# One transfer instead of two for the first step's second pair of q and k, and its split in two operations

## The chip, the cores and the metric

The kernel runs on one core of one Trainium2 chip. The metric is the device time of one execution in microseconds (us); the kernel before takes 1039.08 us, the median of 3 runs (1039.03 to 1039.14). The engines of the core work side by side, each through its own list of instructions in order, and wait for one another through semaphores: PE (TensorE, matrix multiplication; its weight loads are shown apart as PEld), DVE (VectorE, elementwise), ACT (ScalarE, elementwise and functions by table), POOL (GpSimd) and SP (SyncE, which here only issues transfers). Transfers between the chip's main memory and the core's own memory (DMA) are issued by SP or ACT, each into a queue of its own, and carried out by 16 DMA engines.

## The reference

With q, k and v of shape 8 x 12 x 448 x 64 in float32, the attention is a sigmoid one, and its result goes through a feed-forward network with squared ReLU:

```python
scores = scale * np.matmul(q, k.transpose(0, 1, 3, 2)) - np.log(S)
attn = 1.0 / (1.0 + np.exp(-scores))
attn_out = np.matmul(attn, v)
x = np.ascontiguousarray(attn_out.transpose(0, 2, 1, 3)).reshape(B * S, H * D)   # 3584 x 768
h = x @ w_in                       # 768 x 2048
r = np.maximum(h, 0.0)
g = s * (r * r) + b
out = g @ w_out                    # 2048 x 768
```

## The kernel before

The time falls into the attention, the network for a first block of 512 tokens (with weights still being prepared), and the network for two groups of three token blocks each, done by a scheme with fewer block products. Only the start of the attention is touched by the change.

**Steps.** The attention runs over 24 steps, the list `quads`: 8 batches times 3 groups of four heads. One step holds the four heads as two pairs. In a step's tile `x = ld_[0]` of shape [128, 2, 2, 448] the 128 partitions are two heads of 64 dimensions, the second axis is the pair (0 or 1), the third tells q (0) from k (1), the last is the position. So `x[:, 0, 0]` is the first pair's q, `x[:, 0, 1]` its k, `x[:, 1]` the second pair's q and k together, which lie behind one another both in the tile and in main memory: 2 x 448 float32, 3584 bytes a partition.

**High and low parts.** TensorE multiplies plain float32 slowly; a product of numbers rounded to a shorter float32 form (`F32R`) is faster. The kernel therefore splits an operand into a rounded high part and the remainder, the low part, and adds three products, in the order of `PARTS` (line 39): high weights by high data, high weights by low data, low weights by high data. The tiles are `qkh` and `qkl`. They cover, for each pair, the 448 columns of q and the first 384 of k (`NX = S + 3 * P` = 832 columns; `flat` gives this view).

For most steps the split is made by ScalarE (`parts_hi`) and VectorE (`parts_lo`). For the first two steps VectorE makes both (`parts_dve`, lines 390 to 396): for each piece of the list it is given, first a cast (line 394), then a subtraction (line 395, shown in the profile under the helper's line 181).

**Scores.** `scores` (lines 403 to 434) makes six blocks of scores a step: pair `i` in 0, 1 and block `c` in 0 to 2 of 128 positions of k. Each block has two heads, on the two halves of the partitions. In the first step the blocks (0,0) and (0,1) are made of plain float32 straight from the transferred tile (line 426), because the parts aren't there yet; (0,2), (1,0), (1,1) and (1,2) are made in parts (line 420). TensorE takes them in this order. ScalarE makes the sigmoid of each block (line 400). The last 64 positions of k follow later, in `scores_last` (line 441), then the products with v in `attn_v` (line 454) and `attn_v_last` (line 463).

**What is issued first.** `load(..., first=True)` (lines 358 to 368) issues the first step's q and k in five transfers on two queues:

- SP: k of pair 0, the first 128 columns (line 361)
- ACT: q of pair 0 (line 362)
- SP: k of pair 0, the rest (line 363)
- ACT: q of pair 1 (line 364)
- SP: k of pair 1 (line 365)

Then SP issues v of the first step (line 372), q and k of the second step in one transfer (line 367), the first rows of the weights (line 503), v of the second step and two small vectors. ACT, once its transfers are issued, loads its function table and does one tiny operation (line 476). TensorE runs eight warm-up multiplications on constants (line 482, tile `idle`), which need no transfer.

VectorE splits the first step in four pieces (line 594), in this order: q of pair 0; q of pair 1; the last third of pair 0's k that is split (for block (0,2)); k of pair 1. Each piece is a cast and a subtraction, so eight instructions. Tile buffers are in pairs for q and k (`ld`, line 349) and single for the parts (`hl`, line 350).

The order of everything is written out by hand: the loop at line 595 emits the instructions in the order in which each engine takes them, with the preparation of weights placed at given steps (`at_step`, `ticks`).

Of the kernel before, what the change touches and what calls it, by code (L numbers as in the profile page):

```python
# [94 lines left out]
def sigmoid_attention_relu2_ffn(  # L95
# [10 lines left out]
    nc = tc.nc  # L106
    B, NQ, P, _, _, S = qk.shape
# [66 lines left out]
    def f32(ap):  # L174
        return ap.bitcast(F32)
# [4 lines left out]
    def sub(o, x, y):  # L180
        nc.vector.tensor_tensor(o, x, y, op=ALU.subtract)  # L181
# [173 lines left out]
    quads = [(b, t) for b in range(B) for t in range(NQ)]  # L355
    NL = len(quads)

    def load(b, t, first=False):
        x = ld.tile([P, 2, 2, S], F32, tag="qk", name=f"qk_{b}_{t}")
        if first:  # L360
            nc.sync.dma_start(x[:, 0, 1, :P], qk[b, t][:, 0, 1, :P])
            nc.scalar.dma_start(x[:, 0, 0], qk[b, t][:, 0, 0])
            nc.sync.dma_start(x[:, 0, 1, P:], qk[b, t][:, 0, 1, P:])
            nc.scalar.dma_start(x[:, 1, 0], qk[b, t][:, 1, 0])
            nc.sync.dma_start(x[:, 1, 1], qk[b, t][:, 1, 1])
        else:
            nc.sync.dma_start(x, qk[b, t])
        return [x]
# [6 lines left out]
    NX = S + 3 * P  # L375

    def flat(x):
        return x.rearrange("p i x s -> p i (x s)")[:, :, :NX]
# [11 lines left out]
    def parts_dve(b, t, ld_, pieces):  # L390
        hi, lo = (hl.tile([P, 2, NX], F32R, tag=h, name=f"qk{h}_{b}_{t}") for h in "hl")
        x = flat(ld_[0])
        for i, cols in pieces:
            nc.vector.tensor_copy(hi[:, i, cols], x[:, i, cols])
            sub(lo[:, i, cols], x[:, i, cols], f32(hi[:, i, cols]))
        ld_.append((hi, lo))
# [71 lines left out]
    def store_x(b, t, pav):  # L468
        o = xo.tile([P, 2, S], F32, tag="xo", name=f"xo_{b}_{t}")
        nc.vector.tensor_copy(o, pav[:, :, :S])  # L470
        nc.sync.dma_start(x_dram[b][:, 2 * t : 2 * t + 2], o)

    loaded = {0: load(*quads[0], first=True)}
    load_v(*quads[0], loaded[0])
    loaded[1] = load(*quads[1])
    nc.scalar.activation(e_bias, nls, AF.Sigmoid)
    nc.vector.memset(e_bias, -896.0 * 2.0**23)
# [113 lines left out]
    at_step(NL - 2, "ACT", 8, lambda: w1.append(base_hi(0, 0)))  # L591
    at_step(NL - 1, "DVE", 1, lambda: base(0, 0, w1[0]))

    parts_dve(*quads[0], loaded[0], [(0, slice(S)), (1, slice(S)), (0, slice(S + 2 * P, NX)), (1, slice(S, NX))])
    for n, (b, t) in enumerate(quads):
        if n:
            ticks(n, "DVE")
# [15 lines left out]
        if n + 2 < NL:  # L613
            loaded[n + 2] = load(*quads[n + 2])
# [336 lines left out]
    for n, blocks in enumerate(threes):  # L951
# [258 lines left out]
        for j, (i, p) in enumerate(L2):  # L1210
# [8 lines left out]
            for e, tk in LAST if end else [(e, slice(TB)) for e in range(KC)]:  # L1219
# [11 lines left out]
                if end:  # L1231
                    x = C["t"][:, e, tk]
# [57 lines left out]
```

## Time and profile before

| | |
|---|---|
| time, median of 3 runs | 1039.08 us |
| the profiled execution's own time | 1039.04 us |
| its span, first to last instruction | 1037.2 us |
| matrix instructions (PE) | 5290, as many weight loads (PEld) |
| VectorE, ScalarE instructions that count as busy | 910, 666 |
| granted TensorE clock | 1.000 |
| the feed-forward of the two groups of three blocks begins at | 381.35 us |
| shares of the chain by the attention: lines 454, 420, 441, 463 | 11%, 9%, 2%, 2% |

How to read the profile's views. The page gives busy time and share of the span of each engine, and the chain of work that ended last, followed back from the last instruction. The timeline lists instructions in order of time: start in us from the span's start, duration in us, engine, line, operation, the tile written and the tiles read, their shape, the count, and in brackets the idle time of the engine before it and what ended it. An engine name with q (SPq, ACTq) is that engine's issuing of a transfer, which doesn't count as busy; the duration there is that of the issue and not of the transfer. The DMA view gives for each issuing line the size of one transfer and the time from issue to landing. A releaser in brackets is inferred: where several things were waited for it is the one that came last by the profile, and "issue" means that nothing the profile shows was waited for.

### The profile page before, as it was taken

How to read it: one execution, taken by the hardware profiler on the slowest of the kernel's cores; microseconds unless marked ns; L12 is line 12 of the kernel's file. 1: busy time of each engine (PE TensorE's matmuls, PEld its weight loads, DVE VectorE, ACT ScalarE, POOL GpSimd, SP SyncE). 2: the span in 40 equal slices, each digit the busy share in tenths (PEclk: the TensorE clock that was granted, in tenths of full speed). 3: DMA queues.
4: the chain of work that ended last, by engine and by line, in shares of the span. 5: the costliest groups of instructions: out<-in, count | busy, mean ns of one | idle time of the engine just before them, and what ended most of it. 6: DMA issues, size and time to landing. Idle time of an engine off the chain costs nothing.

```text
span 1037.2 us, 13906 instructions
## 1 busy us (share of the span) xinstructions
PE 1033.5 (100%) x5290; PEld 780.9 (75%) x5290; DVE 837.3 (81%) x910; ACT 617.0 (59%) x666; POOL 0.2 (0%) x4
## 2 busy tenths in 40 slices
PE   9999999999999999999999999999999999999998
PEld 4545555555888888888888888888888888888887
DVE  5999999995988965898898897796455789888777
ACT  7999999988776755564445344344445335552432
POOL 0000000000000000000000000000000000000000
PEclk9999999999999999999999999999999999999999
DMA  9788989994999999999686676897666666676773
GB/s 334 265 333 340 359 321 393 345 398 190 338 362 366 358 409 410 340 341 322 201 267 190 218 230 219 292 317 249 197 192 194 194 192 196 191 233 212 221 227 119
DMA packets 101569, 287.17 MB, mean 277 GB/s; under 512 B 10240, under 2 KB 20352, under 8 KB 101504
## 3 DMA queue, kind: packets, MB, share of 16 engines
q1 hardware_dynamic: 101216, 285.84, 79.3%
q8 instruction: 42, 0.69, 0.3%
q10 hardware_dynamic: 288, 0.46, 0.1%
q14 instruction: 23, 0.19, 0.0%
HBM read 198.18 MB, written 88.08 MB: 276 GB/s over the span
## 4 chain that ended last, share of the span: by engine, by line
PE 100%; DVE 0%; issue 0%
PE o L1225 31%; PE h L1095 31%; PE pav L454 11%; PE psc L420 9%; PE ph L563 6%; PE po L765 6%; PE psc_l L441 2%; PE pav L463 2%; PE idle L482 0%; PE psc L426 0%; DVE C_t L181 0%
## 5 line engine op out<-in xcount | busy, mean ns | idle before, releaser
L1095 PE MATMUL h<-s_0h,wu 128*128 128x512 f32 x480 | 148.0, 389 | 0.0
L1095 PE MATMUL h<-s_1h,wu 128*128 128x512 f32 x480 | 147.8, 389 | 0.0
L400 ACT ACTIVATE a<-psc,nls 128x896 f32<-128x896 f32 x144 | 132.7, 1008 | 12.9 <-PE psc L420 10.1
L454 PE MATMUL pav<-a,v 128*64 128x448 f32 x576 | 113.8, 543 | 0.0
L1095 PEld LDWEIGHTS h<-s_0h,wu 128*128 128x128 f32 x480 | 90.1, 188 | 18.8
L1095 PEld LDWEIGHTS h<-s_1h,wu 128*128 128x128 f32 x480 | 90.1, 188 | 18.6
L968 ACT COPY G<-h 128x1024 f32<-128x1024 f32 x48 | 48.8, 1017 | 85.4 <-PE h L1095 57.7
L860 ACT ACTIVATE G<-G,b_sb,s_sb 128x1024 f32<-128x1024 f32 x48 | 59.8, 1246 | 61.4 <-DVE G L857 60.7
L1095 PE MATMUL h<-s_0l,wu 128*128 128x512 f32 x240 | 93.4, 389 | 0.0
L1095 PE MATMUL h<-s_1l,wu 128*128 128x512 f32 x240 | 93.4, 389 | 0.0
L454 PEld LDWEIGHTS pav<-a,v 128*64 128x64 f32 x576 | 39.1, 137 | 63.8 <-issue 45.4
L178 DVE TENSOR_TENSOR G<-G,h 128x1024 f32<-128x1024 f32 x40 | 48.8, 1219 | 39.1 <-PE h L1095 38.9
L1225 PE MATMUL o<-g_3h,wu 128*128 128x512 f32 (+1 forms) x244 | 79.0, 385 | 0.0
L1225 PE MATMUL o<-g_1h,wu 128*128 128x512 f32 x240 | 78.8, 389 | 0.0
L1225 PE MATMUL o<-g_2h,wu 128*128 128x512 f32 x240 | 78.8, 389 | 0.0
L1225 PE MATMUL o<-g_0h,wu 128*128 128x512 f32 x240 | 78.8, 389 | 0.0
L765 PE MATMUL po<-g,w 128*128 128x512 f32 x288 | 67.7, 389 | 0.0
L765 PEld LDWEIGHTS po<-g,w 128*128 128x128 f32 x288 | 54.1, 188 | 11.2
L563 PE MATMUL ph<-x0h,w 128*128 128x512 f32 x192 | 61.7, 390 | 0.0
L420 PE MATMUL psc<-qkh 64*128 64x448 f32 x284 | 54.8, 382 | 0.0
L1225 PEld LDWEIGHTS o<-g_3h,wu 128*128 128x128 f32 x244 | 45.6, 188 | 9.2
L1225 PEld LDWEIGHTS o<-g_0h,wu 128*128 128x128 f32 x240 | 45.1, 188 | 9.4
(152 smaller groups left out, 2029.7 us busy)
## 6 DMA issues: line engine op xcount, KB each, us to landing
wu<-wd SPq DMA_DIRECT2D x240, 512.0 KB, 3.8
wd<-t SPq DMA_DIRECT2D x36, 768.0 KB, 8.1
qk<-qk_t SPq DMA_DIRECT2D x23, 896.0 KB, 7.1
st<-w_out SPq DMA_DIRECT2D x16, 768.0 KB, 9.3
st<-w_in SPq DMA_DIRECT2D x16, 768.0 KB, 9.2
wd<-w SPq DMA_DIRECT2D x16, 768.0 KB, 5.9
v<-v_t SPq DMA_DIRECT2D x24, 448.0 KB, 5.4
xd<-xo SPq DMA_DIRECT2D x24, 448.0 KB, 4.4
```

Source lines behind the costliest of these rows:

```text
L178: nc.vector.tensor_tensor(o, x, y, op=ALU.add)
L400: nc.scalar.activation(a, psc[:, :, :S], AF.Sigmoid, bias=nls, scale=SCALE)
L420: nc.tensor.matmul(o[:, j, :S], two[wi][r, i, cols], two[xi][r, i, :S], start=m == 0, stop=m == 2,)
L441: nc.tensor.matmul(psc[half[i], j, :S], x[r, i, 1, 3 * P :], x[r, i, 0, :], start=True, stop=True,)
L454: nc.tensor.matmul(pav[r, i, :S], ld_[1][:, 3 * i + c, j, :], a[i, c][:, j, :], start=c == 0, stop=False,)
L463: nc.tensor.matmul(pav[r, i, :S], ld_[1][half[i], 6, j, :], a[half[i], j, :], start=False, stop=True,)
L563: nc.tensor.matmul(ph, w[:, k, wi, kc * P : (kc + 1) * P], x0[h][xi][:, cc, :], start=m == 0, stop=m == 3 * NCC - 1,)
L765: nc.tensor.matmul(pos[e], w[:, k, wi, kc * P : (kc + 1) * P], g[:, gi, :], start=first and i == 0, stop=last and i == 2,)
L860: nc.scalar.activation(x, x, AF.Identity, bias=b_sb, scale=s_sb)
L968: nc.scalar.copy(g(m, h), bk)
L1095: nc.tensor.matmul(bk[:, j], wt[:, j, wi, c * P : (c + 1) * P], opd[i][xi][:, c, :], start=i == ch[0] and m == 0, stop=m == 3 * KC - 1, sk ...
L1225: nc.tensor.matmul(o, wt[:, f, wi, e * P : (e + 1) * P], g[gi][:, f, tk], start=(end or i == ch[0] and p == 0) and f == 0 and m == 0, stop ...
```

## The change

In `load`, the two transfers of pair 1 (q on ACT's queue, k on SP's) become one transfer of `x[:, 1]`, both, on SP's queue, at the place where k of pair 1 was. ACT's queue keeps q of pair 0 alone. In the split on VectorE, the piece for block (0,2) moves ahead of pair 1, and pair 1's two pieces become one of 832 columns: three pieces, six instructions.

```diff
@@ -361,8 +361,7 @@
             nc.sync.dma_start(x[:, 0, 1, :P], qk[b, t][:, 0, 1, :P])
             nc.scalar.dma_start(x[:, 0, 0], qk[b, t][:, 0, 0])
             nc.sync.dma_start(x[:, 0, 1, P:], qk[b, t][:, 0, 1, P:])
-            nc.scalar.dma_start(x[:, 1, 0], qk[b, t][:, 1, 0])
-            nc.sync.dma_start(x[:, 1, 1], qk[b, t][:, 1, 1])
+            nc.sync.dma_start(x[:, 1], qk[b, t][:, 1])
         else:
             nc.sync.dma_start(x, qk[b, t])
         return [x]
@@ -591,7 +590,7 @@
     at_step(NL - 2, "ACT", 8, lambda: w1.append(base_hi(0, 0)))
     at_step(NL - 1, "DVE", 1, lambda: base(0, 0, w1[0]))
 
-    parts_dve(*quads[0], loaded[0], [(0, slice(S)), (1, slice(S)), (0, slice(S + 2 * P, NX)), (1, slice(S, NX))])
+    parts_dve(*quads[0], loaded[0], [(0, slice(S)), (0, slice(S + 2 * P, NX)), (1, slice(NX))])
     for n, (b, t) in enumerate(quads):
         if n:
             ticks(n, "DVE")
```

The arithmetic of every element is the same. Behind line 364 the line numbers of the changed kernel are one smaller.

## The prediction

> **What bounds the kernel now.** I read the first page from the top: busy times first, then the chain of work that ended last.
>
> ```profile
> span 1037.2 us, 13906 instructions
> PE 1033.5 (100%) x5290; PEld 780.9 (75%) x5290; DVE 837.3 (81%) x910; ACT 617.0 (59%) x666; POOL 0.2 (0%) x4
> PE 100%; DVE 0%; issue 0%
> ```
>
> The reader is to see that TensorE is the bound over the whole span: it is busy for 1033.5 of 1037.2 us and the chain is all PE. So the change can move the end only by moving a time at which TensorE starts or waits; time saved or lost on VectorE, ScalarE or a queue counts only where TensorE stood behind it. Conversely, a stall of TensorE near the start is not made up later, because no slack stands behind it in the chain.
>
> The change touches the first 8 us alone, so the second view is the chain restricted to the first 40 us.
>
> ```profile
> 0.77 3.15 PE idle L482 x8
> 3.92 2.98 PE psc L426 x8
> 6.90 2.43 PE psc L420 x24
> 9.33 2.41 PE pav L454 x12
> ```
>
> The first column is the start, the second the duration. The eight warm-up matmuls (`idle`) run to 3.92, the plain fp32 scores of blocks (0,0) and (0,1) to 6.90, the scores in parts, (0,2) and (1,0) to (1,2), to 9.33, then attention times v. Each piece starts where the one before ends: TensorE never stops between 0.77 and 9.33. The question is whether each instruction's operands still arrive in time.
>
> Third, the timeline of the first 3 us: who issues which transfer (start, duration of the issue, queue).
>
> ```profile
> 0.72 0.41 ACTq L362 DMA_DIRECT2D qk<-qk_t  x1
> 0.73 0.38 SPq L361 DMA_DIRECT2D qk<-qk_t  x1
> 1.16 0.45 ACTq L364 DMA_DIRECT2D qk<-qk_t  x1
> 1.17 0.42 SPq L363 DMA_DIRECT2D qk<-qk_t  x1
> 1.64 0.42 SPq L365 DMA_DIRECT2D qk<-qk_t  x1
> 1.65 1.28 ACT L476 ACT_TABLE_LOAD   x1 [1.65 <-PEq L1280]
> 2.10 0.43 SPq L372 DMA_DIRECT2D v<-v_t  x1
> ```
>
> L362 is the first q (q0), L361 and L363 the two pieces of the first k (k0a, 128 columns; k0b, the rest), L364 the second q (q1), L365 the second k (k1). Fourth, the DMA view restricted to the first 2.5 us: size of each and time from issue to landing.
>
> ```profile
> qk<-qk_t ACTq DMA_DIRECT2D x2, 224.0 KB, 3.2
> v<-v_t SPq DMA_DIRECT2D x1, 448.0 KB, 5.3
> qk<-qk_t SPq DMA_DIRECT2D x1, 224.0 KB, 4.1
> qk<-qk_t SPq DMA_DIRECT2D x1, 160.0 KB, 3.5
> qk<-qk_t SPq DMA_DIRECT2D x1, 64.0 KB, 2.6
> ```
>
> With the issue times: k0a lands at 0.73 + 2.6 = 3.33, k0b at 1.17 + 3.5 = 4.67, k1 at 1.64 + 4.1 = 5.74, v at 2.10 + 5.3 = 7.40. Fifth, VectorE, which splits q and k into high and low parts.
>
> ```profile
> 3.58 0.40 DVE L394 CAST qkh<-qk 128x448 fp32r<-128x448 f32 x1 [0.32 <-DMA qk<-qk_t]
> 4.01 0.62 DVE L181 TENSOR_TENSOR qkl<-qk,qkh 128x448 fp32r<-128x448 f32 x1
> 4.82 0.40 DVE L394 CAST qkh<-qk 128x448 fp32r<-128x448 f32 x1 [0.18 <-DMA qk<-qk_t]
> 5.25 0.62 DVE L181 TENSOR_TENSOR qkl<-qk,qkh 128x448 fp32r<-128x448 f32 x1
> 5.79 0.22 DVE L394 CAST qkh<-qk 128x128 fp32r<-128x128 f32 x1
> 6.04 0.29 DVE L181 TENSOR_TENSOR qkl<-qk,qkh 128x128 fp32r<-128x128 f32 x1
> 6.25 0.35 DVE L394 CAST qkh<-qk 128x384 fp32r<-128x384 f32 x1
> 6.64 0.56 DVE L181 TENSOR_TENSOR qkl<-qk,qkh 128x384 fp32r<-128x384 f32 x1
> 9.77 0.59 DVE L394 CAST qkh<-qk 128x832 fp32r<-128x832 f32 x1 [2.58 <-DMA qk<-qk_t]
> 10.40 1.03 DVE L181 TENSOR_TENSOR qkl<-qk,qkh 128x832 fp32r<-128x832 f32 x1
> ```
>
> The pairs are q0, q1, the last third of k0 used by (0,2), and k1. The last two rows are half of the next step's split: a cast and a subtraction of 832 columns, exactly the form that the change makes of the q1 and k1 pairs. Last, the weight loads of TensorE, which show when the operands are needed.
>
> ```profile
> 4.75 0.34 PEld L426 LDWEIGHTS psc<-qk 64*128 64x128 f32 x2 [0.41 <-DMA qk<-qk_t]
> 5.50 0.34 PEld L426 LDWEIGHTS psc<-qk 64*128 64x128 f32 x2 [0.41 <-issue]
> 6.25 0.30 PEld L420 LDWEIGHTS psc<-qkh 64*128 64x128 f32 x2 [0.41 <-DVE qkh L394]
> 6.74 0.19 PEld L420 LDWEIGHTS psc<-qkl,qkh 64*128 64x128 f32 x2 [0.19 <-issue]
> 6.94 0.19 PEld L420 LDWEIGHTS psc<-qkh,qkl 64*128 64x128 f32 x2
> 7.14 0.19 PEld L420 LDWEIGHTS psc<-qkh 64*128 64x128 f32 x2
> 7.34 0.20 PEld L420 LDWEIGHTS psc<-qkl,qkh 64*128 64x128 f32 x2
> 7.54 0.20 PEld L420 LDWEIGHTS psc<-qkh,qkl 64*128 64x128 f32 x2
> ```
>
> The loads at 4.75, 5.50 and 6.25 stand 0.75 us apart, each after the same 0.41 of idle time, though three releasers are named. The one in the middle waited for nothing the profile shows, so 0.75 is TensorE's own pace for an fp32 round, and the DMA and VectorE named at the other two had just come in time. The three loads from 6.25 are (0,2); those at 7.14, 7.34 and 7.54 are (1,0): high by high, high weights against low q, low weights against high q. After that the pace is 0.20 us a round.
>
> **The change, part by part.** All sums stand against the profiled execution's own 1039.04 us (span 1037.2, 1.84 around it), 0.04 under the median of 1039.08 of the runs.
>
> *ScalarE's queue loses the transfer at 1.16.* It saves 0.45 us of issue there, so the table load may begin at about 1.2 instead of 1.65. Worth nothing, because ScalarE's first real work waits for TensorE:
>
> ```profile
> 5.76 1.01 ACT L400 ACTIVATE a<-psc,nls 128x896 f32<-128x896 f32 x1 [2.62 <-PE psc L426]
> 6.95 4.60 ACT L400 ACTIVATE a<-psc,nls 128x896 f32<-128x896 f32 x5 [0.19 <-PE psc L426]
> ```
>
> The cover is the 2.62 us of idle time before 5.76. Without it the saving could count for at most its 0.45 us.
>
> *SyncE's queue.* The third transfer carries 448 KB instead of 224. Its issue should cost the same: 0.42 us for 224 KB at 1.64, 0.43 for v's 448 KB at 2.10. So v and everything issued behind it (the next step's q and k, the weight rows) is issued when it was. The bytes ahead of v are the same, so v still lands near 7.40, before attention times v at 9.33; cover 1.9 us.
>
> *When does the joint transfer land?* It is not in the trace; this is the disputed term. From below, k0b's 3.5 us give 1.64 + 3.5 = 5.14. From above, v, issued just behind it, landed 5.3 us after its issue; the same for the joint transfer gives 1.64 + 5.3 = 6.94. I take 4.1 us, that of k1, hence 5.74: k1 was issued at that very place, and when it had landed the same bytes as now had to be in: 64 + 160 + 224 on SyncE's queue and twice 224 on ScalarE's, 896 KB. The change reorders them and takes none away.
>
> One page of the Trainium skill says otherwise. "DMA: Bandwidth & Descriptors", section "Anatomy of one DMA — SWDGE (gpsimd) path", gives a transfer as 2.0 us fixed plus its bytes at 436 GB/s. It is stated for the other path's transfers; an estimate by it is 2.0 + 1.05 = 3.05 us for 448 KB, a landing at 4.69, and then the sum below would be zero. The trace does not bear it out for transfers queued behind others: the same estimate for k1's 224 KB is 2.5 us, and its row has 4.1.
>
> *VectorE's order.* New order: q0 (high, low), the last third of k0, then q1 and k1 as one cast and one subtraction of 832 columns. q0 ends at 4.01 + 0.62 = 4.63, k0b is in at 4.67, so the k0 third runs from about 4.7 to 4.7 + (6.33 - 5.79) = 5.24 instead of 6.33. TensorE gains nothing, since (0,2) cannot start before its own pace lets it, at 6.25. Four instructions become two, and 0.40 + 0.62 + 0.35 + 0.56 = 1.93 us become 0.59 + 1.03 = 1.62. That saving is also off the path: after this VectorE waits 2.58 us for the next q and k until 9.77, and neither the bytes ahead of that transfer nor its issue time change.
>
> *The new wait.* Before, the low part of q1 was ready at 5.87, and k1's at 6.64 + 0.56 = 7.20, asked for at 7.54. Now both come out of one subtraction, so the load at 7.34 waits for it. From the rows at 9.77 and 10.40, cast start to end of the subtraction is 0.63 + 1.03 = 1.66; the cast starts some 0.02 to 0.1 after landing. Landing at 5.74 gives 5.79 + 1.66 = 7.45, against a need at 7.34. High parts are no concern (5.79 + 0.59 = 6.38, needed at 7.14). TensorE then waits 7.45 - 7.34 = 0.11 us. What stands behind it on TensorE are the rest of (1,0), (1,1), (1,2) and attention times v, all in its own order, so all of them move by 0.11. ScalarE does not: its third and fourth sigmoids follow one another in the run of five from 6.95, at about 0.92 us each, the fourth of all at 6.95 + 2 x 0.92 = 8.8 for (1,0), which TensorE, with its last weight load at 7.54 and 0.20 us a round, ends near 8.0; cover some 0.7 us. SyncE's next load into this tile waits for the later subtraction too, but also for TensorE's last scores from the tile, which stand behind attention times v in TensorE's order and so come later.
>
> Sum: 0 (queues) + 0 (saved VectorE time) + 0 ((0,2) earlier) + 0.11 (new wait) = +0.11 us, hence 1039.04 + 0.11 = 1039.15. By the bounds of the landing time the wait is 0 (landing 5.14: the subtraction ends at 6.85) to 8.65 - 7.34 = 1.31 us (landing 6.94).
>
> **Rivals.** *A: no wait at all.* If the joint transfer lands before 5.63 (7.34 less 1.66 and 0.05), TensorE never sees it: 1039.04. For it speaks that 5.63 is within 0.11 us of my 5.74, and half as many, longer rows might move a little faster; against it, that k1 at the same place needed 4.1 us. Should the joint transfer in fact be cut into the same pieces as before, so that nothing differs but the queue, the time is this one too.
>
> *B: slower, a late landing.* The one subtraction now stands behind the last byte of both halves, so any delay of that transfer goes one to one into TensorE from a landing at 5.63 on. If it takes as long as v did, the wait is 1.31 us and the time 1040.35. For it: v's row shows that 448 KB on this queue at this time did need 5.3 us; against it: v lay behind all 896 KB, the joint transfer is the end of them. It decides as slower by over 0.2% only if the landing came at 5.63 + 2.08 = 7.71, beyond v's own.
>
> *C: faster, an earlier start.* With q1 gone from ScalarE's queue, q0 and k0b have less beside them. If TensorE's first scores waited for q0 (its load at 3.84 does name a DMA), they start earlier, and everything with them:
>
> ```profile
> 3.84 0.51 PEld L426 LDWEIGHTS psc<-qk 64*128 64x128 f32 x4 [0.73 <-DMA qk<-qk_t]
> ```
>
> ScalarE's two transfers have 3.2 us in the middle; q1, which VectorE saw at 4.82, took some 3.6 from 1.16, so q0 took about 2.8 and landed at 0.72 + 2.8 = 3.52. The most that rival C can give is q0 as early as k0a, at 3.33: 0.19 us, so 1038.85. Against it: VectorE saw q0 at 3.58, a quarter of a microsecond before that load, and the warm-up matmuls hold TensorE to 3.92 anyhow. k0b coming earlier gives nothing, as its load at 4.75 was at TensorE's pace. The rule behind this rival is in the same page of the Trainium skill, section "Queues, rings and completion order": each DMA engine takes turns between the queues that have work, so one queue less leaves larger shares to the other. No row here shows the turns themselves.
>
> **How the numbers follow.** Forecast (a wait of 0.02 to 0.6 us): 0.53. Rival A: 0.30, as its bound is so near. Rival B (over 0.6 us): 0.09. Rival C: 0.08. The range takes in the forecast's waits, A and C, each with the spread of the runs (1039.03 to 1039.14): 1038.8 to 1039.8; what it leaves out is B and a little of what nobody named. Faster or slower by over 0.2%, which is 2.08 us and about what a measurement of this kernel can tell from no change, would need a landing after 7.71 or a start earlier by ten times what C offers: 0.01 and 0.03, and 0.96 for within it.
>
> **What would show it.** In the profile after: three issues on SyncE's queue at 0.73, 1.17 and 1.64 and one on ScalarE's; the table load near 1.2; the k0 third's cast near 4.7; one cast of 832 columns at the landing plus 0.02 to 0.1, with idle time before it put down to the DMA; the second and third rounds of (0,2) at 6.74 and 6.94 as before; and the low-q round of (1,0) at 7.34 plus the wait, its load naming the subtraction. A landing before 5.63 without a wait is A. I am wrong if TensorE's rounds before 7.14 move, if the wait is over 0.6 us, or if the time moves by more than the first 10 us account for.

## The result and the profile after

The changed kernel is slower: 1040.45 us, the median of 21 runs (1039.80 to 1041.37), against 1038.86 for the kernel before (21 runs, 1038.45 to 1040.25). The ratio is 1.0016 with a 95% interval of 1.001 to 1.0022. That is within the 0.2% named in the prediction, but outside the range of 1038.8 to 1039.8. The profiled execution took 1040.38 us, 1.34 more than the one of before, where the forecast was 0.11.

The first page: TensorE is still nearly all of the chain, but a transfer has entered it.

```profile
span 1038.6 us, 13902 instructions
PE 1034.1 (100%) x5290; PEld 780.6 (75%) x5290; DVE 837.0 (81%) x908; ACT 617.1 (59%) x666; POOL 0.2 (0%) x4
PE 99%; DMA 0%; DVE 0%; SPq 0%; issue 0%
```

The chain of the first 40 us (start, duration) shows where:

```profile
1.58 0.05 issue
1.64 5.02 DMA qk<-qk_t
6.65 0.02 issue
6.68 0.61 DVE qkh L393
7.28 0.02 issue
7.31 1.04 DVE qkl L181
8.34 0.04 issue
8.39 1.91 PE psc L419 x15
10.30 2.41 PE pav L453 x12
```

Where the chain of before ran along TensorE from the first warm-up, this one runs from the issue of the joint transfer at 1.64 through its landing at 6.65, the cast and the subtraction to TensorE at 8.39. The products with v begin at 10.30 for 9.33: 0.97 us is lost here.

The transfers of the first 2.5 us, size and time to landing:

```profile
qk<-qk_t SPq DMA_DIRECT2D x1, 448.0 KB, 5.0
v<-v_t SPq DMA_DIRECT2D x1, 448.0 KB, 6.5
qk<-qk_t ACTq DMA_DIRECT2D x1, 224.0 KB, 2.8
qk<-qk_t SPq DMA_DIRECT2D x1, 160.0 KB, 2.8
```

k0b lands sooner than before (2.8 us for 3.5); the joint transfer takes 5.0, where k1 at the same place took 4.1. VectorE's new order and TensorE's weight loads:

```profile
4.53 0.22 DVE L393 CAST qkh<-qk 128x128 fp32r<-128x128 f32 x1
6.68 0.60 DVE L393 CAST qkh<-qk 128x832 fp32r<-128x832 f32 x1 [1.61 <-DMA qk<-qk_t]
7.31 1.03 DVE L181 TENSOR_TENSOR qkl<-qk,qkh 128x832 fp32r<-128x832 f32 x1
```

```profile
6.12 0.19 PEld L419 LDWEIGHTS psc<-qkh 64*128 64x128 f32 x2 [0.28 <-issue]
6.49 0.19 PEld L419 LDWEIGHTS psc<-qkl,qkh 64*128 64x128 f32 x2 [0.19 <-issue]
6.70 0.18 PEld L419 LDWEIGHTS psc<-qkh,qkl 64*128 64x128 f32 x2
7.39 0.22 PEld L419 LDWEIGHTS psc<-qkh 64*128 64x128 f32 x2 [0.51 <-PE psc L419]
8.39 0.19 PEld L419 LDWEIGHTS psc<-qkl,qkh 64*128 64x128 f32 x2 [0.78 <-DVE qkl L181]
```

VectorE waits 1.61 us for the transfer, and the low-q round of (1,0) names the subtraction, at 8.39 where it had stood at 7.34. The low-part rounds of block (0,2) run 0.25 us earlier than before (6.49 and 6.70 for 6.74 and 6.94), which the prediction had excluded.

A second loss stands far from the change. ScalarE's first sigmoid of the fifth step, in the profile of before and then of after:

```profile
48.20 3.73 ACT L400 ACTIVATE a<-psc,nls 128x896 f32<-128x896 f32 x4 [0.58 <-PE psc L420]
```

```profile
49.48 1.91 ACT L399 ACTIVATE a<-psc,nls 128x896 f32<-128x896 f32 x2 [0.89 <-PE psc L419]
```

It starts 1.28 us later than before, though TensorE is only 0.97 late there (its scores of that step begin at 48.27 for 47.30). TensorE then waits for ScalarE (0.30 us in the scores, 0.39 before the products) and ends up about 0.35 us later still: its main stage, the feed-forward of the two groups, begins at 382.67 for 381.35, so 1.32 of the 1.34 us.

### The profile page after: what moved, and what is told of

Read it like the earlier page. It is cut to its first block, busy times and chain, and to the rows that moved or that the text cites. A ratio compares the mean times of both kernels' runs of the same rounds, so it can differ in the third digit from the quotient of the medians.

```text
span 1038.6 us, 13902 instructions
## 1 busy us (share of the span) xinstructions
PE 1034.1 (100%) x5290; PEld 780.6 (75%) x5290; DVE 837.0 (81%) x908; ACT 617.1 (59%) x666; POOL 0.2 (0%) x4
## 4 chain that ended last, share of the span: by engine, by line
PE 99%; DMA 0%; DVE 0%; SPq 0%; issue 0%
PE o L1224 31%; PE h L1094 31%; PE pav L453 11%; PE psc L419 9%; PE ph L562 6%; PE po L764 6%; PE psc_l L440 2%; PE pav L462 2%; DMA qk<-qk_t 0%; DVE qkl L181 0%; DVE qkh L393 0%; DVE C_t L181 0%; SPq L363 0%; SPq L361 0%
## 5 line engine op out<-in xcount | busy, mean ns | idle before, releaser
L419 PE MATMUL psc<-qkl,qkh 64*128 64x448 f32 x284 | 52.0, 363 | 0.5 <-DVE qkl L181 0.5
```

Of the source, the lines that this page charges most:

```text
L419: nc.tensor.matmul(o[:, j, :S], two[wi][r, i, cols], two[xi][r, i, :S], start=m == 0, stop=m == 2,)
```

## The experiments

Asked in turn: is it the transfer or the split; what makes the transfer late; is that accident or rule; what the loss at 49 us is. "Products" is the start of the first products with v in the timeline: 9.27 before, 10.23 after.

**The split alone** (transfers as before).

```diff
-    parts_dve(..., [(0, slice(S)), (1, slice(S)), (0, slice(S + 2 * P, NX)), (1, slice(S, NX))])
+    parts_dve(..., [(0, slice(S)), (0, slice(S + 2 * P, NX)), (1, slice(NX))])
```

> Transfers as before (five, two queues), the split on VectorE as after (q0, the third of k0, then q1 and k1 in one cast and one subtraction). Two theories of the lost time. S: the joint transfer is late because its first rows of 3584 bytes start slowly, as v's did in the trace before. Q: it is late because everything now stands in one queue. Both say here that nothing of the lateness is left: k1 lands some 4.1 us after its issue (5.7), the joint subtraction ends at 7.4, the products with v begin between 9.1 and 9.4 (before 9.27, after 10.23), and the time is within 0.2 us of before. A rival to both, that the joint split itself costs the time: the products begin after 9.8.

k1 took 4.3 us (landing 5.94), the subtraction ended at 7.65, and the products began at 9.53, a little past the 9.4 expected: landing, 1.66 of VectorE, and TensorE, the prediction's sum with 0.2 us more of landing. Median 1039.33, ratio 1.0004 (0.9995 to 1.0013): not told from no change. So the split is not what costs the 0.97 us. It is not free either: here TensorE's low-q round waited for the joint subtraction, to 7.71, and the products stood 0.26 us later than before.

**The transfer alone** (split as before).

```diff
-            nc.scalar.dma_start(x[:, 1, 0], qk[b, t][:, 1, 0])
-            nc.sync.dma_start(x[:, 1, 1], qk[b, t][:, 1, 1])
+            nc.sync.dma_start(x[:, 1], qk[b, t][:, 1])
```

> The joint transfer on SyncE's queue as after, VectorE's four pieces in the order of before (q0, q1, third of k0, k1). What is asked is whether the landing is late with the old split too, and what the new order saves. The transfer lands 4.8 to 5.2 us after its issue (6.4 to 6.8); the third of k0 now stands behind q1, so block (0,2) waits for the transfer as well: its low part comes 1.5 us after the landing and k1's 0.8 to 0.9 later. The products with v begin at 10.4 to 10.9 (after 10.23). A rival, that the joint split had made the transfer's cost worse: they begin before 10.1.

Landing after 4.9 us, products at 10.63, 1040.71 us, ratio 1.0018 (1.0008 to 1.0028). The whole loss comes with the transfer; the new split, in one profile of each, gives 0.4 us of it back, as (0,2) no longer stands behind q1 on VectorE.

**Two transfers on SyncE's queue.**

```diff
-            nc.sync.dma_start(x[:, 1], qk[b, t][:, 1])
+            nc.sync.dma_start(x[:, 1, 0], qk[b, t][:, 1, 0])
+            nc.sync.dma_start(x[:, 1, 1], qk[b, t][:, 1, 1])
```

> As after, but q1 and k1 are two transfers of 224 KB one behind the other on SyncE's queue (rows of 1792 bytes); ScalarE's queue has q0 alone; v is issued one place later. S: the rows are small, so no slow start: k1, issued at 2.1, lands at 5.3 to 5.9, and the products with v begin at 9.0 to 9.4; time within 0.3 us of before. Q: one queue is what is slow: k1 lands at 6.3 to 7.0, the products begin at 9.9 to 10.5; time 0.7 to 1.6 us above before.

**The joint transfer on ScalarE's queue.**

```diff
-            nc.sync.dma_start(x[:, 1], qk[b, t][:, 1])
+            nc.scalar.dma_start(x[:, 1], qk[b, t][:, 1])
```

> As after, but the joint transfer is issued on ScalarE's queue behind q0, at 1.16, where q1 was. S: rows of 3584 bytes start slowly wherever they stand: landing about 5 us after the issue, 6.1 or later, and the products with v begin at 9.7 or later. Q: two queues are in use again, so it lands as q1 and k1 did before, 4.8 to 5.6, and the products begin at 9.0 to 9.3.

S falls twice; Q's landings hold both times. With small rows but one queue, k1 landed at 2.10 + 4.71 = 6.81 and the products began at 10.44 (1040.64 us, ratio 1.0016, 1.0007 to 1.0025). With the large rows on ScalarE's queue the transfer landed 3.9 us after its issue, and VectorE began with it at once (the chain's transfer of 3.95 from 1.17, the cast):

```profile
1.17 3.95 DMA qk<-qk_t
5.11 0.02 issue
5.14 0.60 DVE qkh L393
```

Products at 8.66, 1038.83 us, ratio 1.0 (0.999 to 1.0009): the loss is gone. That they began earlier than Q's 9.0 is TensorE's pace in this profile (last section), and the median shows no gain. What the DMA engines moved shows the difference too. Each row is half a microsecond: the busy time of PE, PEld, DVE, ACT and POOL, then the granted clock, the DMA share and GB/s; first after, then this kernel:

```profile
3.50:4.00 0.50, 0.50 (x4) 0.16 (x2) 0.41 (x2) 0.00 (x0) 0.00 (x0) 1.00 1.03 206
4.00:4.50 0.50, 0.50 (x2) 0.35 (x4) 0.50 (x1) 0.00 (x0) 0.00 (x0) 1.00 1.01 280
4.50:5.00 0.50, 0.50 (x4) 0.25 (x2) 0.47 (x3) 0.00 (x0) 0.00 (x0) 1.00 0.79 201
```

```profile
3.50:4.00 0.50, 0.50 (x4) 0.16 (x2) 0.39 (x1) 0.00 (x0) 0.00 (x0) 1.00 1.06 423
4.00:4.50 0.50, 0.50 (x2) 0.35 (x4) 0.48 (x1) 0.00 (x0) 0.00 (x0) 1.00 0.99 401
4.50:5.00 0.50, 0.50 (x6) 0.27 (x4) 0.47 (x3) 0.00 (x0) 0.00 (x0) 1.00 1.06 430
```

After moves bytes at about half the rate, while the DMA engines are nearly as busy: the packets took longer (112 from 3.5 to 5.0 us in after, 213 in this kernel). The joint transfer alone is not the reason, for the kernel before slows down too, one microsecond later:

```profile
4.50:5.00 0.50, 0.50 (x4) 0.24 (x2) 0.32 (x2) 0.00 (x0) 0.00 (x0) 1.00 1.68 283
5.00:5.50 0.50, 0.50 (x2) 0.10 (x2) 0.47 (x2) 0.00 (x0) 0.00 (x0) 1.00 0.51 179
```

In both kernels the stretch begins when ScalarE's queue has run dry: the DMA view shows no packet of it from 4.5 us on in before and from 3.5 us on in after. The Trainium skill, "DMA: Bandwidth & Descriptors", section "Issuing engines are not separate DMA queues", says that issuing from several engines saves only the issue time, as all share the same DMA engines. Here the issue was 0.47 us earlier and the landing 1.5 us (5.12 for 6.65), so more than the issue time was saved in these first microseconds. Whether the other queue did it is not shown by this kernel alone: the transfer also stands second in its queue and no longer third. The experiments on the place in the queue, below, take that up.

**The third of k0 earlier, four pieces** (transfers as before).

```diff
-    parts_dve(..., [(0, slice(S)), (1, slice(S)), (0, slice(S + 2 * P, NX)), (1, slice(S, NX))])
+    parts_dve(..., [(0, slice(S)), (0, slice(S + 2 * P, NX)), (1, slice(S)), (1, slice(S, NX))])
```

> Transfers as before; VectorE's four pieces as before but the third of k0 stands ahead of q1: q0, third of k0, q1, k1. In the trace after block (0,2) ran 0.25 us earlier than before (low-part rounds at 6.69 for 6.94). If that was the earlier third of k0, the products with v begin at 9.0 to 9.1 here (before 9.27) and the time is 0.1 to 0.4 us under before. If my step stands that (0,2) was at TensorE's own pace, they begin at 9.27 and the time is the same. Both S and Q say the transfers land as before.

Products at 9.24, 1038.76 us, ratio 0.9999 (0.999 to 1.0007): no gain, so the step that (0,2) is held by TensorE's own pace stands. That its rounds stood 0.25 earlier in after is then a change of that pace (see the repeat of before below).

**The place in the queue.** Four kernels change what stands ahead of the joint transfer, or beside it. The first brings k0 in one transfer:

```diff
-            nc.sync.dma_start(x[:, 0, 1, :P], qk[b, t][:, 0, 1, :P])
+            nc.sync.dma_start(x[:, 0, 1], qk[b, t][:, 0, 1])
             nc.scalar.dma_start(x[:, 0, 0], qk[b, t][:, 0, 0])
-            nc.sync.dma_start(x[:, 0, 1, P:], qk[b, t][:, 0, 1, P:])
```

> As after, but k0 comes in one transfer, so that the joint transfer is the second of SyncE's queue and not the third, issued at 1.17. Two theories of what is slow in one queue. D: each transfer of 128 rows takes some 1.1 to 1.3 us of its queue's time, few bytes or many, so the place in the queue decides: the joint transfer lands about 1.2 us earlier than after (6.65), near 5.4, and the products with v begin before 9.4. L: a queue that works alone, once q0 is done near 3.3, moves slowly whatever stands before: the landing stays about 5.0 us after the issue or later, 6.2 to 6.6, and the products begin at 9.8 or later.

Landing after 4.2 us, at 5.37, as D has it, not L. That is 0.25 us after the landing on ScalarE's queue (5.12), with the same issue time and the same place, so in one profile of each the place counts for more than the queue. The products came only at 10.59 all the same, which D had not expected: beside the whole k0 (3.4 us) q0 on the other queue needed 3.6 us for 2.8, TensorE waited for q0 and began at 4.41 for 3.84, and its plain rounds kept the pace of 0.75 us to the end. The median is 1039.64 us (ratio 1.001, 1.0 to 1.0019); the profiled execution took 1040.77.

The second brings k0's rest in two transfers:

```diff
-            nc.sync.dma_start(x[:, 0, 1, P:], qk[b, t][:, 0, 1, P:])
+            nc.sync.dma_start(x[:, 0, 1, P : 2 * P], qk[b, t][:, 0, 1, P : 2 * P])
+            nc.sync.dma_start(x[:, 0, 1, 2 * P :], qk[b, t][:, 0, 1, 2 * P :])
```

> As after, but k0's rest comes in two transfers (128 and 192 columns), so that the joint transfer is the fourth of SyncE's queue, issued at 2.1, with the same bytes ahead. D: it lands 1.0 to 1.3 us later than after, 7.6 to 8.0, and the products with v begin at 11.1 to 11.6. L: only the issue moves by 0.47; it lands at 6.6 to 7.1 and the products begin at 10.2 to 10.7.

Landing after 5.1 us at 7.22, products at 10.77, 1040.88 us (ratio 1.0019, 1.001 to 1.0029). Outside both: one small transfer more ahead cost 0.57 us against after, 0.46 of it the issue. Against the 6.14 of after's second profile (below) it would be 1.08, so a single profile of each does not settle D's price of a transfer.

The third issues the first v on ScalarE's queue (`load_v` is given the queue as an argument for it):

```diff
-    load_v(*quads[0], loaded[0])
+    load_v(*quads[0], loaded[0], nc.scalar)
```

> As after, but the first step's v is issued on ScalarE's queue behind q0, so that a second queue has work while the joint transfer, third of SyncE's queue as after, is under way. D: its place is the same, so it lands as after, 6.2 to 6.8, and the products with v begin near 10.2. L: two queues work, so it lands as the same transfer did on ScalarE's queue, or as k1 before, 5.1 to 5.8, and the products begin before 9.5.

Landing after 4.7 us (6.38), products at 9.94, 1039.86 us (ratio 1.001, 1.0001 to 1.002). As D has it: a second busy queue did not help a transfer at this place, and L falls. The rate was back, 430, 403 and 416 GB/s from 3.5 to 5.0 us, but with v's bytes among them; v landed after 4.1 us.

The fourth takes the step's q and k in one:

```diff
-    loaded = {0: load(*quads[0], first=True)}
+    loaded = {0: load(*quads[0])}
```

> As after, but the first step's q and k (896 KB) come in one transfer on SyncE's queue, issued first; ScalarE's queue has nothing. Asked is what a single queue can do with a single transfer. D (what counts is how many transfers stand ahead in the queue): it moves at the full rate from the start, the windows from 2.5 to 4.5 us show 350 to 420 GB/s, and it lands 4.2 to 4.7 us after its issue, at 4.9 to 5.4, earlier than the joint half did in after (6.65). L (a queue alone is slow): the windows show 200 to 300 GB/s and it lands at 6.0 or later. TensorE's first scores wait for all of it, so the time is no measure here.

896 KB landed 4.4 us after the issue, sooner than the 448 KB of after, and the windows from 3.5 to 4.5 are full (the one execution took 1041.43 us):

```profile
3.50:4.00 0.50, 0.41 (x2) 0.00 (x0) 0.00 (x0) 0.00 (x0) 0.00 (x0) 1.00 1.03 430
4.00:4.50 0.50, 0.00 (x0) 0.00 (x0) 0.00 (x0) 0.00 (x0) 0.00 (x0) 1.00 1.03 416
```

So a single queue is not slow by itself. What the four show: on SyncE's queue q and k come 4.4 us after the issue as first transfer (896 KB), 4.2 as second, 4.5 to 5.0 as third, 5.1 as fourth (448 KB each), and on ScalarE's, as second, 3.9. Why the third moves so slowly, no view shows. The low rate begins where ScalarE's queue runs dry, but an empty second queue is not enough for it: here, and with k0 in one transfer (401, 323 and 380 GB/s from 4.0 to 5.5 us), SyncE's queue worked alone and was faster than in after. Neither theory's numbers hold throughout, and the cause stays open.

**Both kernels again**, unchanged, one execution of each.

> The kernel before, a second profile. In the profiles so far TensorE's plain fp32 rounds change their pace from 0.75 to 0.38 us at different times, 4.3 to 8 us from the start. If that differs from execution to execution, with the same instructions, it changes at another time than at 6.2 to 6.9 here, and the products with v begin up to 0.3 us earlier than 9.27 if it comes earlier. If it belongs to the kernel, the rounds stand at 3.85, 4.75, 5.50 and 6.25 again.

> The kernel after, a second profile. If the late landing belongs to the queue, the joint transfer lands 4.7 to 5.1 us after its issue again and the products with v begin between 9.9 and 10.3 whatever the pace of TensorE's first rounds. If 5.0 was one execution's accident, it lands near 5.74 and they begin near 9.4.

Before: products at 9.08, k1 after 3.9 us, 1038.85 us. The same instructions ran at another pace: the weight loads stood at 5.50, 6.14, 6.51 where they had stood at 5.50, 6.25, 6.74.

```profile
5.50 0.34 PEld L426 LDWEIGHTS psc<-qk 64*128 64x128 f32 x2 [0.41 <-issue]
6.14 0.19 PEld L420 LDWEIGHTS psc<-qkh 64*128 64x128 f32 x2 [0.30 <-DVE qkh L394]
6.51 0.19 PEld L420 LDWEIGHTS psc<-qkl,qkh 64*128 64x128 f32 x2 [0.19 <-issue]
```

After: landing after 4.5 us (6.14), the low-q round at 7.87, products at 9.68, 1039.81 us. Later than k1's 5.74, but less late than the first time, and outside both expectations. The loss is smaller too: 0.60 us at the products and 0.88 at the main stage (382.04 for 381.16). So the landing varies by half a microsecond from execution to execution; in four profiles with the transfer at this place (after twice, the transfer alone, and the next kernel) it took 4.5, 4.9, 5.0 and 5.0.

**One instruction more on ScalarE.**

```diff
     nc.scalar.activation(e_bias, nls, AF.Sigmoid)
+    nc.scalar.activation(e_bias, nls, AF.Sigmoid)
```

> As after, with ScalarE's tiny first operation on one column issued twice, so that ScalarE's list is again as long as before (it lost one transfer's issue). In all six profiles of kernels whose list is one shorter than before, the first sigmoid of the fifth step waits 0.89 us; in the six whose list has the old length, and in the one that is two shorter, 0.58; TensorE is 0.3 us later for it from about 52 us on. If the length of the list is what does it, the idle time before that sigmoid is 0.58 here, TensorE's lateness against before is the same at 47 and at 55 us, and the time is some 0.3 us under after's (1040.45). If it comes from the late start itself, it is 0.89 again. The head is as in after: landing 4.5 to 5.0 us after the issue.

```profile
49.14 3.73 ACT L399 ACTIVATE a<-psc,nls 128x896 f32<-128x896 f32 x4 [0.58 <-PE psc L419]
```

The idle time is 0.58 again, as expected if the length of the list does it, with TensorE as late in the head as in after (landing after 5.0 us, products at 10.16). Its lateness against before is 0.97 us at the second step's products with v (21.53 for 20.56) and 0.98 at the main stage (382.33 for 381.35), so the extra 0.35 is gone. 1040.05 us, ratio 1.0014 (1.0004 to 1.0024); the medians differ by 0.4 from after's, too little to be told by times alone. The kernel with v on ScalarE's queue agrees: its list has the old length, it is 0.67 us late at the products, and the idle time is 0.58. So the second loss comes with the length of ScalarE's list, one less by the removed issue, and not from the late start. Why one less makes that sigmoid 0.31 late, and two less (the kernel with one transfer) does not, is open.

## Why the prediction was wrong

The step that failed is "I take 4.1 us, that of k1, hence 5.74". Its reason was that the same 896 KB had to be in. The bytes were the same; their place in the queues was not, nor the rate. Before, half of the pair's bytes came through ScalarE's queue as its second transfer, and the DMA engines moved 384 and 382 GB/s from 3.5 to 4.5 us; now all come as SyncE's third, at 206 and 280 in the same stretch, and took 5.0 us, 4.5 to 5.0 over the four profiles. What makes the rate fall is open. The upper bound, v's 5.3 us, held, and rival B, given 0.09, is what happened: its price of 1.31 us for a landing at 6.94 stands beside 0.97 for one at 6.65.

The mechanism behind the term held. The cast began 0.02 to 0.06 us after the landing in after, in its repeat and in the split alone; the subtraction ended 1.66 later (7.31 + 1.03 = 8.34 in after), and only the low-q round waited decisively. With 5.0 in the place of 4.1 the prediction's own sum gives 6.65 + 0.03 + 1.66 - 7.34 = 1.00 us, against the 0.97 lost in the head. That "what stands behind moves by as much" held too: 0.97 from 10.30 on.

Point by point: the issues at 0.73, 1.17 and 1.64, the table load at 1.16 (near 1.2 expected) and the k0 third at 4.53 (near 4.7) were right. The issue removed from ScalarE's list was priced at nothing; in the head that is true, but it cost about 0.35 us through the sigmoid at 49 us, which no part of the working had looked for. v landed at 8.60 and not 7.40, the same step failing again (bytes ahead taken for time), but still before it was used. "The rounds at 6.74 and 6.94 as before" was wrong, by TensorE's pace; the second profile of before misses it too (6.51 for 6.74), so these rounds were no sign of the change. Rival C, an earlier start, did not come: the first load stands at 3.84 in both. Rival A's missing wait did not come either.

## What to carry to other kernels

Joining two transfers that stood on two queues is not neutral because the bytes are: ask for the place of each in its queue, and price it from the nearest transfer of that place and size (here v's 5.3 us, one place later) rather than from the smaller one that it replaces. An instruction that waits for a joint transfer, and a joint operation behind it, put the last byte of both halves on the path, so such a joint is worth trying where slack stands behind it. Moving the same joint transfer to the other queue, where it was issued 0.47 us sooner and stood second, took the whole loss away, but won nothing over the kernel before.

## What the hardware showed beside

TensorE's pace at the start differs from execution to execution. The plain fp32 rounds stood 0.75 us apart in the profile of before, and with the same instructions 0.38 from 4.54 on where the joint transfer was on ScalarE's queue:

```profile
4.54 0.19 PEld L425 LDWEIGHTS psc<-qk 64*128 64x128 f32 x2 [0.20 <-DMA qk<-qk_t]
4.92 0.19 PEld L425 LDWEIGHTS psc<-qk 64*128 64x128 f32 x2 [0.19 <-issue]
5.30 0.19 PEld L419 LDWEIGHTS psc<-qkh 64*128 64x128 f32 x2 [0.19 <-DVE qkl L181]
```

The granted clock in the windows is 1.00 all the while, so this is to be read from the spacing alone. The Trainium skill, "TensorE: Matmul & The Clock Gate", section "Part 1: The HAM clock gate", has the array at half its clock until it has been busy for a window of about 3.4 us whose phase is free; the trace agrees with the halving and with a time that differs between executions. So one profile of the head is worth some tenths of a microsecond and not hundredths: in the kernel before, the products with v began at 9.27 and at 9.08.
